# Loads two double pairs ahead, copies in the tick of their matmul, and a held-back second set in a long-convolution and FFN kernel

## The chip, the cores and the metric

The kernel runs on one core of a Trainium2 chip. The metric is the device time of one execution in microseconds (us); the profile shows one execution by its engines: TensorE (PE, its weight loads apart as PEld), VectorE (DVE), ScalarE (ACT), GpSimd (POOL), and the DMA issues of SyncE (SP) and GpSimd.

## The reference

For four sequences of 12480 positions and 128 channels, a long convolution by FFT is followed by a product and by a feed-forward network (FFN):

```python
h_filt = (np.maximum(pos_emb @ w1, 0.0) @ w2) * np.exp(-0.01 * np.arange(S))[:, None]
Uf = np.fft.rfft(x * v, n=2 * S, axis=1)
Hf = np.fft.rfft(h_filt, n=2 * S, axis=0)
y = np.fft.irfft(Uf * Hf[None], n=2 * S, axis=1)[:, :S]
t = (x * y).reshape(B * S, 128)
h = t @ w_in                      # 128 -> 2048
out = (h / (1 + np.exp(-1.702 * h))) @ w_out
```

## The kernel before

The transform is written as two stages of matmuls with constant matrices, and its inverse likewise. The work on the convolution comes in five sets (SETS: which block and which one or two of the sequences); set 0 also computes the filter's spectrum.

Stage 1 of a set takes 26 pairs of columns. For a pair it multiplies x and v (L226), computes two columns of the filter by a small network (mlp_in L192, Relu L194 into rt, mlp_out L200, product with the window L202), adds and subtracts (fold, L182 and L183), multiplies by a constant matrix (L242), copies the result from PSUM (a, L245) and stores it to the DRAM tensor g_d (g_out, L208). Two neighbouring pairs form a double pair and share their loads: x2 (L214), f2 (L217) and pt (L187).

Stage 2 of a set takes 31 steps v. A step loads two column groups from g_d (L315), multiplies by the small matrix wf (forward, L302), copies spectra to eu (L334), forms the products t1 and t2 on VectorE (L340) and y on GpSimd (L344, L345), multiplies by wv (inverse, L308), copies to z (L356) and stores to z_d (L357). Set 0's spectra are needed by the later sets. The eu tiles of the last KEEP steps have buffers of their own, and spec_store (L360, L361) writes them to DRAM after the loop; those of the first steps share two buffers and are stored in the loop.

The third part (p3_unit) loads z_d by GpSimd's queue (zt L456, vt L460, x3 L462), does the last inverse matmul (L482) and the product with x, and leaves the FFN's input as two parts xh and xl. The FFN runs over 104 halves (NH) of 8 steps. A step has six matmuls of 480 columns into h (L555), two Gelu passes (L556, L557), a subtraction (L563) and six matmuls into acc (L572).

What sets the order: the program order is written out by hand, each engine keeps it, and so does each DMA queue. A unit of work is a Python generator. One tick of a Pipe advances every live generator by one yield, the oldest first, and then the new one. So a statement that stands n yields deep in a generator is issued n ticks after its unit began. In the prologue there is one tick for each pair of stage 1 and each step of stage 2 of set 0, with five and nine empty ticks behind them, and every tick ends with two heat matmuls (L625, their result is unused). Buffers are rings: the n-th tile of a tag takes the place of the (n - bufs)-th and waits for its last reader. All wide PSUM results of set 0 take a ring of three (cv2), and the small network has a single bank.

After the prologue the other sets are fed between the FFN's steps by Feed: every unit has a weight, pace(k, span) sets the weight per step so that a mark (the end of a set) is reached in span steps, and run(steps) issues units up to that goal. `begin[0]` is the step at which the first half of set 1 needs its z_d, 96. Ahead of the first FFN step six ticks of the third part run.

The pools of the prologue (st, and keep for the eu tiles) are closed behind it, and the pools of the FFN (ffn) and of the fed sets (main) take that memory.

Of the kernel before, what the change touches and what calls it, by code (L numbers as in the profile page):

```python
# [9 lines left out]
F32 = mybir.dt.float32  # L10
F32R = mybir.dt.float32r
U32 = mybir.dt.uint32
ACTF = mybir.ActivationFunctionType
# [11 lines left out]
M = HALF // N2  # L25
K1 = N1 // 2 + 1
KP = 128
KZ = 122
NP = N2 // 2
# [4 lines left out]
WCH = 512  # L34
LAG = 4
STEPS = FC // 2
KEEP = 22

PAIRS = [(n, N2 - n) for n in range(1, NP)] + [(0, NP)]
SETS = [(0, 0, 1), (0, 1, 1), (0, 2, 2), (1, 0, 2), (1, 2, 2)]  # L40
# [72 lines left out]
def conv_ffn_kernel(  # L113
# [45 lines left out]
    def sb(name, shape, dt, bufs, tag=None, where="s"):  # L159
        return ps[where].tile(shape, dt, tag=tag or name, bufs=bufs, name=name)  # L160
# [15 lines left out]
    def flat(t):  # L176
        return t.rearrange("p a b c -> p (a b c)")
# [7 lines left out]
    def mlp_load(j, p):  # L185
        pt = sb("pt", [128, 2 * M], F32, 2)
        nc.sync.dma_start(out=pt, in_=posm[:, j, p // 2])  # L187
        return pt
# [16 lines left out]
    def g_out(j, p, a):  # L205
        for q in range(2):
            r = 64 * q + 2 * p
            nc.sync.dma_start(out=g_d[j][r:r + 2].rearrange("r k c -> k r c"), in_=a[:, :, q * 256:(q + 1) * 256])  # L208

    def p1_start(p):  # L210
        c, h = divmod(p, 2)
        if h == 0:
            x2 = sb("x2", [M, 2, 2, 2, 128], F32, 4, "g")
            nc.sync.dma_start(out=x2, in_=xv[:, 8 * c:8 * c + 8].rearrange("m (p x i) d -> m p x i d", p=2, x=2))  # L214
            f2 = sb("f2", [M, 3, 2, 128], F32, 2)
            n = 3 if p + 1 == LONE else 2
            nc.sync.dma_start(out=f2[:, 0:n], in_=c_f0[:, p:p + n])  # L217
            shared["in"] = x2, f2, mlp_load(0, p)
        x2, f2, pt = shared["in"]
        yield  # L220
        if h == 0:
            shared["rt"] = mlp_in(pt)
        rt = shared["rt"]
        yield
        u = sb("u", [M, 2, 2, 128], F32, 2)
        tt(out=u[:, :, 1], in0=x2[:, h, 0], in1=x2[:, h, 1], op=ALU.mult)  # L226
        mlp_out(u, rt, 0, p)
        yield
        if p == LONE:
            pq = u  # L230
        else:
            pq = sb("pq", [M, 2, 2, 128], F32, 2)
            fold(pq, u)
        yield
        t, bs = pair(True)
        for ri in range(2):
            if p == LONE:
                for q in range(2):
                    mm(out=bs[ri][:, q * 256:(q + 1) * 256], lhsT=f2[:, h + ri, q],
                       rhs=pq[:, ri].rearrange("p b c -> p (b c)"), start=True, stop=True)  # L240
            else:
                mm(out=bs[ri], lhsT=f2[:, h, ri], rhs=flat(pq), start=True, stop=True)  # L242
        yield
        a = sb("a", [KP, 2, 512], F32, 2)
        act(a, t, ACTF.Copy)  # L245
        yield
        g_out(0, p, a)

# [71 lines left out]
    def p2_start(v):  # L320
        nw = min(2, KZ // 2 - 2 * v)
        w0 = 2 * v
        wd = 128 * nw
        g = p2_load(0, v, nw)
        yield
        yield
        t, xy = pair(True)
        forward(g, nw, xy)
        yield
        keep = v >= NV - KEEP  # L330
        eu = sb("eu", [128, 2, 2, 2, 128], F32, KEEP if keep else 2, where="k" if keep else "s")
        tv = t[:, :, 0:256 * nw].rearrange("p l (w s c) -> p s w l c", w=nw, s=2)
        for s in range(2):
            act(eu[:, s, 0:nw], tv[:, s], ACTF.Copy)  # L334
        yield
        t1 = sb("t1", [128, 2, wd], F32, 2, "u")
        t2 = sb("t2", [128, 2, wd], F32, 2, "pq")
        pw = [128, 2, nw, 128]
        for i, to in enumerate((t1, t2)):
            tt(out=to.rearrange("p l (w c) -> p l w c", w=nw), in0=tv[:, 1].rearrange("p w l c -> p l w c"),  # L340
               in1=eu[:, 0, 0:nw, i].unsqueeze(1).broadcast_to(pw), op=ALU.mult)
        yield
        y = sb("y", [128, 2, wd], F32, 2)
        nc.gpsimd.tensor_tensor(out=y[:, 0], in0=t1[:, 0], in1=t2[:, 1], op=ALU.subtract)  # L344
        nc.gpsimd.tensor_tensor(out=y[:, 1], in0=t2[:, 0], in1=t1[:, 1], op=ALU.add)  # L345
        if keep:
            spectra.append((eu, w0, nw))
        else:
            spec_store(eu, w0, nw)
        yield  # L350
        yield
        t, ab = pair(True)
        inverse([y[:, i].rearrange("p (w c) -> p w c", w=nw) for i in range(2)], nw, wd, ab)
        yield
        z = sb("z", [128, 2, 2, 128], F32, 2)
        act(z[:, 0:nw].rearrange("p w a c -> p a w c"), t[:, :, 0:wd].rearrange("p a (w c) -> p a w c", w=nw), ACTF.Copy)  # L356
        nc.sync.dma_start(out=z_d[0][:, 4 * v:4 * v + 2 * nw, :], in_=z[:, 0:nw].rearrange("p w a c -> p (w a) c"))  # L357

    def spec_store(eu, w0, nw):
# [243 lines left out]
    with tc.manual_schedule():  # L603
        with tc.tile_pool(name="ps0", bufs=3, space=PSUM) as ps0, tc.tile_pool(name="ps0b", bufs=1, space=PSUM) as ps0b, \
                tc.tile_pool(name="st", bufs=1) as st, tc.tile_pool(name="keep", bufs=1) as kp:
            ps["s"], ps["k"] = st, kp
            ps["p"] = type("P", (), {"tile": staticmethod(
                lambda shape, dt, tag, name: (ps0 if tag == "cv2" else ps0b).tile(shape, dt, tag=tag, name=name))})
            warm = sb("warm", [128, 512], mybir.dt.bfloat16, 1)
            nc.vector.memset(warm, 0.0)  # L610
            zero = sb("zero", [128, KP - KZ, 256], F32, 1)
            nc.vector.memset(zero, 0.0)
            nc.vector.memset(w1_sb, 0.0)
            nc.vector.memset(w2_sb, 0.0)
            nc.vector.memset(sgn_sb[0:64], 1.0)
            nc.vector.memset(sgn_sb[64:128], -1.0)
            for h in range(2):
                nc.sync.dma_start(out=w1_sb[64 * h:64 * h + 64, 64 * h:64 * h + 64], in_=w1)
                nc.sync.dma_start(out=w2_sb[64 * h:64 * h + 64, h], in_=w2)
            nc.sync.dma_start(out=win_sb, in_=c_win)  # L620
            wb = ps0b.tile([128, 512], F32, tag="wb", name="wb")

            def heat(k):
                for _ in range(k):
                    mm(out=wb, lhsT=warm[:, 0:128], rhs=warm, start=True, stop=True)  # L625

            heat(24)
            pipe, wpipe = Pipe(), Pipe()
            wu = list(weight_units())
            units = [p1_start(p) for p in range(NP)] + [None] * 5  # L630
            units += [p2_start(v) for v in range(NV)] + [None] * 9
            for n, u in enumerate(units):
                pipe.tick(u)
                heat(2)
                if n == 4:
                    nc.sync.dma_start(out=wf, in_=c_wf)
                    nc.sync.dma_start(out=wv, in_=c_wi)
                    for o in range(5):
                        nc.sync.dma_start(out=z_d[o][:, KZ:KP], in_=zero[:, :, 0:128 * SETS[o][2]])
                if n >= 5:  # L640
                    wpipe.tick(wu.pop(0) if n % 6 == 5 and wu else None)
            assert not wu and not wpipe.live and not pipe.live
            for sp in spectra:
                spec_store(*sp)
# [9 lines left out]
        first = {next(i for i, hv in enumerate(HV) if hv[0] == o): o for o in range(1, 5)}  # L654
        begin = sorted(when(n) for n in first)
        feed = Feed(pipe, *conv_feed())
        feed.pace(0, begin[0])
        for n in range(6):
            p3.tick(p3_unit(0) if n == 0 else None)
            feed.run(1)  # L660
        ffn = Ffn()
        pend = []
        for n in range(NH):
            for k in range(STEPS):
                if pend:
                    ffn.lo(pend[-1])
                if len(pend) == LAG - 1 and pend[0][1] == STEPS - 1:
                    ffn.mm2(pend.pop(0))
                pend.append(ffn.mm1(n, k))
                feed.run(0.5)  # L670
                if n + 1 < NH:
                    new = None
                    if k == 0:
                        if n + 1 in first:
                            o = first[n + 1]
                            feed.reach()
                            if o < 4:
                                feed.pace(o, begin[o] - begin[o - 1] - 2)
                            else:
                                feed.rate = 0.0  # L680
                        new = p3_unit(n + 1)
                    p3.tick(new)
                if k == 4:
                    ffn.store()
                if len(pend) == LAG:
                    ffn.mm2(pend.pop(0))
                feed.run(0.5)
        ffn.lo(pend[-1])
        for it in pend:
            ffn.mm2(it)  # L690
# [124 lines left out]
```

## Time and profile before

| | |
|---|---|
| median of 3 runs | 3180.36 us (3177.92 to 3182.05) |
| profiled execution, time | 3184.23 us |
| profiled execution, span | 3182.5 us |
| mean granted TensorE clock | 0.972 |
| PE busy | 3025.1 us, 95% |
| DMA moved | 541.84 MB |
| SP queue's share of 16 DMA engines | 38.8% |
| GpSimd queue's share | 15.6% |

The span runs from the first to the last instruction. A busy share is a mean over stretches that differ much: the first 351 us hold set 0's two stages and the hand-over, the rest the FFN with the other sets fed between its steps. Matmuls are pipelined, so a busy PE may still be late by small amounts. A wait is put down to what ended last before the waiting instruction began.

### The profile page before, as it was taken

To read this page: it belongs to the slowest core of one execution; us is meant where nothing else is said; L and a number is where in the kernel's file an instruction comes from. 1 tells how busy PE (TensorE), PEld (TensorE's weight loads), DVE (VectorE), ACT (ScalarE), POOL (GpSimd) and SP (SyncE) were. 2 spreads that over 40 slices of the span, in tenths; PEclk is the share of its full clock that TensorE was granted. 3 is DMA by queue.
4 is the path that set the end of the run, shared out by engine and by line. 5 is a ranking of instruction groups with operands and counts; after the bars stand their busy time and mean duration, and the time that the engine had idled before them with its cause. 6 is when DMAs were issued, how large, how long until landed. Compare 5 with 4: busy or idle time off the path is not lost.

```text
span 3182.5 us, 42011 instructions
## 1 busy us (share of the span) xinstructions
PE 3025.1 (95%) x15191; PEld 2313.3 (73%) x15206; DVE 2156.1 (68%) x2874; ACT 2073.1 (65%) x2812; POOL 426.4 (13%) x694
## 2 busy tenths in 40 slices
PE   6764699999999999999999999999999999999999
PEld 3311587668866678877777887777777888888887
DVE  3452467777777776799998548888887444545444
ACT  1233576668877777766666766666666767666676
POOL 0033111012201011111111111111111111111110
PEclk7877899999999999999999999999999999999999
DMA  6676888889977797665656524544542111111110
GB/s 194 196 235 201 247 243 263 248 254 316 313 236 255 241 295 214 187 201 195 197 185 189 158 80 131 169 152 162 169 159 88 49 54 48 54 47 54 47 55 26
DMA packets 281799, 541.84 MB, mean 170 GB/s; under 512 B 30963, under 2 KB 149811, under 8 KB 281595
## 3 DMA queue, kind: packets, MB, share of 16 engines
q1 hardware_dynamic: 230603, 390.34, 38.8%
q0 software_dynamic: 50992, 148.82, 15.6%
q8 instruction: 123, 2.02, 0.3%
q14 instruction: 81, 0.66, 0.1%
HBM read 330.24 MB, written 208.80 MB: 169 GB/s over the span
## 4 chain that ended last, share of the span: by engine, by line
PE 43%; issue 39%; POOL 4%; DVE 2%; SPq 1%; DMA 1%; ACT 0%; POOLq 0%; DVEq 0%; ACTq 0%
PE acc L572 15%; PE h L555 15%; PE cv L302 3%; PE cv L482 3%; PE cv L308 2%; POOL zt L456 2%; PE cv L172 1%; PE cv L174 1%; PE cv L173 1%; POOL out_dram L583 1%; POOL x L462 1%; POOL vt L460 1%; SPq L360 1%; SPq L361 1%; DVE fgl L563 0%
## 5 line engine op out<-in xcount | busy, mean ns | idle before, releaser
L563 DVE TENSOR_TENSOR fgl<-fg,fgh 128x960 fp32r<-128x960 f32 x832 | 959.1, 1155 | 603.0 <-ACT fg L557 530.7
L556 ACT ACTIVATE fgh<-h 128x960 fp32r<-128x960 f32 x832 | 810.3, 974 | 587.7 <-PE h L555 586.4
L555 PE MATMUL h<-xh,wi 128*128 128x480 f32 x3328 | 1130.8, 383 | 0.0
L572 PE MATMUL acc<-fgh,wo 128*128 128x480 f32 x3328 | 884.8, 387 | 0.0
L557 ACT ACTIVATE fg<-h 128x960 f32<-128x960 f32 x832 | 807.1, 970 | 9.3 <-DVE fgl L563 9.2
L555 PEld LDWEIGHTS h<-xh,wi 128*128 128x128 f32 x3328 | 626.0, 188 | 184.4 <-issue 67.2
L572 PEld LDWEIGHTS acc<-fgh,wo 128*128 128x128 f32 x3328 | 609.6, 188 | 172.9 <-issue 86.0
L555 PE MATMUL h<-xl,wi 128*128 128x480 f32 x1664 | 632.2, 380 | 0.0
L572 PE MATMUL acc<-fgl,wo 128*128 128x480 f32 x1664 | 500.3, 382 | 1.7 <-DVE fgl L563 1.7
L572 PEld LDWEIGHTS acc<-fgl,wo 128*128 128x128 f32 x1664 | 312.8, 188 | 51.4 <-DVE fgl L563 2.1
L555 PEld LDWEIGHTS h<-xl,wi 128*128 128x128 f32 x1664 | 312.9, 188 | 47.4
L583 POOL DMA_DIRECT2D out_dram<-ot x104 | 57.1, 549 | 2009.8 <-ACT ot L576 2007.6
L482 PEld LDWEIGHTS cv<-vt,zt 122*128 122x128 f32 x1664 | 202.1, 193 | 20.8 <-ACT fg L557 6.5
L482 PE MATMUL cv<-vt,zt 122*128 122x120 f32 x1664 | 205.4, 277 | 2.5 <-DMA vt<-in_c_v_dram 1.6
L302 PE MATMUL cv<-g,wf 52*64 52x512 f32 (+1 forms) x1240 | 182.3, 640 | 9.1 <-DMA g<-g_d 4.9
L456 POOL DMA_DIRECT2D zt<-z_d x208 | 151.7, 735 | 15.5 <-DMA e_d<-eu 6.9
L440 ACT ACTIVATE z<-cv 128x512 f32<-128x512 f32 (+2 forms) x248 | 120.5, 545 | 41.7 <-PE cv L308 41.4
L492 DVE TENSOR_TENSOR a<-cv,yq 128x240 f32<-128x240 f32 (+1 forms) x101 | 40.7, 403 | 140.8 <-ACT yq L490 85.1
L295 ACT ACTIVATE a<-cv 128x512 f32<-128x512 f32 x208 | 120.9, 607 | 23.2 <-PE cv L174 21.3
L308 PE MATMUL cv<-t,wv 52*64 52x512 f32 (+2 forms) x992 | 126.2, 555 | 2.7 <-DVE e L420 1.7
L262 POOL DMA_DIRECT2D ft<-in_c_f_dram x108 | 57.5, 534 | 479.5 <-PE cv L174 444.7
L576 ACT ACTIVATE ot<-acc 128x480 f32<-128x480 f32 x104 | 59.5, 572 | 91.4 <-PE acc L572 91.4
(84 smaller groups left out, 2514.5 us busy)
## 6 DMA issues: line engine op xcount, KB each, us to landing
g_d<-a SPq DMA_DIRECT2D x260, 256.0 KB
g<-g_d SPq DMA_DIRECT2D x300, 208.0 KB
zt<-z_d POOLq DMA_DIRECT2D x208, 256.0 KB, 4.3
e<-e_d SPq DMA_DIRECT2D x180, 256.0 KB
z_d<-z SPq DMA_DIRECT2D x90, 512.0 KB
xt<-in_xv_dram SPq DMA_DIRECT2D x78, 480.0 KB
u<-us_d SPq DMA_DIRECT2D x60, 512.0 KB
ft<-in_c_f_dram POOLq DMA_DIRECT2D x108, 240.0 KB, 4.5
```

The lines of the kernel that those rows point to most:

```text
L295: act(a[:, ri], b, ACTF.Copy)
L302: mm(out=xy[q ^ c][64 * c:64 * c + 64, 0:256 * nw].rearrange("p (w c) -> p w c", w=nw), lhsT=wf[64 * q:64 * q + N2, c], rhs=g[64 * q:64 * ...
L308: mm(out=ab[h][64 * pl:64 * pl + 64, 0:w].rearrange("p (w c) -> p w c", w=nw), lhsT=wv[64 * h:64 * h + N2, pl], rhs=y[pl ^ h][64 * h:64 * ...
L440: act(zv[:, :, h], ab[h][:, 0:wd].rearrange("p (w c) -> p w c", w=nw), ACTF.Copy)
L456: q.dma_start(out=zv[:, gq], in_=z_d[o][64 * gq + 2 * p0:64 * gq + 2 * p0 + 2 * npr].rearrange("r k c -> k r c"))
L482: mm(out=b[:, c0:c0 + M], lhsT=lhs, rhs=rhs, start=(k == 0), stop=(k == 1))
L555: mm(out=h[:, i, 0:TW], lhsT=wt[:, s], rhs=xx, start=st, stop=sp)
L556: act(gh, h[:, :, 0:TW], ACTF.Gelu_apprx_sigmoid)
L557: act(gf, h[:, :, 0:TW], ACTF.Gelu_apprx_sigmoid)
L563: tt(out=gl, in0=gf, in1=gh.bitcast(F32), op=ALU.subtract)
L572: mm(out=acc, lhsT=wt[:, 2 * k + i, :], rhs=xx[:, i], start=(t == 0 and i == 0 and k == 0), stop=(t == 2 and i == 1 and k == STEPS - 1))
L583: nc.gpsimd.dma_start(out=out[:, n], in_=ot)
```

## The change

- Stage 1 of set 0: the loads of a double pair become p1_load and are issued AHEAD = 2 double pairs before their first use; two of them are issued ahead of the loop. pt is now loaded first. The rings: pt 3 in place of 2, f2 5 smaller ones in place of 2; the third matrix that the last pair needs gets a tile of its own, f3.
- The copy of a is issued in the tick of its matmul; its store stays in the tick where it was.
- Stage 2 of set 0: the copy to eu is issued in the tick of the forward matmul, and all that follows it one tick earlier; the copy to z is issued in the tick of the inverse matmul, and its store one tick after. z has three buffers in place of two.
- KEEP is 21 in place of 22, and the tile of zeros is one row that the stores to z_d broadcast six times.
- HOLD = 10: no unit of set 1 is issued in the six ticks ahead of the FFN and in its first ten steps, and set 1's pace is reckoned over 86 steps.

```diff
-KEEP = 22
+KEEP = 21
+AHEAD = 2
+HOLD = 10
...
+    def p1_load(c):
+        p = 2 * c
+        pt = sb("pt", [128, 2 * M], F32, 3)
+        nc.sync.dma_start(out=pt, in_=posm[:, 0, c])
+        x2 = sb("x2", [M, 2, 2, 2, 128], F32, 4, "g")
+        nc.sync.dma_start(out=x2, in_=xv[:, 8 * c:8 * c + 8].rearrange("m (p x i) d -> m p x i d", p=2, x=2))
+        f2 = sb("f2", [M, 2, 2, 128], F32, 5)
+        nc.sync.dma_start(out=f2, in_=c_f0[:, p:p + 2])
+        fl = [f2[:, 0], f2[:, 1]]
+        if p + 1 == LONE:
+            f3 = sb("f3", [M, 2, 128], F32, 1)
+            nc.sync.dma_start(out=f3, in_=c_f0[:, NP])
+            fl.append(f3)
+        shared["in", c] = x2, fl, pt
+
     def p1_start(p):
         c, h = divmod(p, 2)
-        if h == 0:
-            x2 = sb("x2", [M, 2, 2, 2, 128], F32, 4, "g")
...
-            f2 = sb("f2", [M, 3, 2, 128], F32, 2)
...
-            shared["in"] = x2, f2, mlp_load(0, p)
-        x2, f2, pt = shared["in"]
+        if h == 0 and c + AHEAD < NP // 2:
+            p1_load(c + AHEAD)
+        x2, fl, pt = shared["in", c]
         yield
...
-                mm(out=bs[ri], lhsT=f2[:, h, ri], rhs=flat(pq), start=True, stop=True)
-        yield
+                mm(out=bs[ri], lhsT=fl[h][:, ri], rhs=flat(pq), start=True, stop=True)
         a = sb("a", [KP, 2, 512], F32, 2)
         act(a, t, ACTF.Copy)
+        yield
         yield
         g_out(0, p, a)
...
         forward(g, nw, xy)
-        yield
         keep = v >= NV - KEEP
...
         inverse([y[:, i].rearrange("p (w c) -> p w c", w=nw) for i in range(2)], nw, wd, ab)
-        yield
-        z = sb("z", [128, 2, 2, 128], F32, 2)
+        z = sb("z", [128, 2, 2, 128], F32, 3)
         act(z[:, 0:nw].rearrange("p w a c -> p a w c"), t[:, :, 0:wd].rearrange("p a (w c) -> p a w c", w=nw), ACTF.Copy)
+        yield
         nc.sync.dma_start(out=z_d[0][:, 4 * v:4 * v + 2 * nw, :], in_=z[:, 0:nw].rearrange("p w a c -> p (w a) c"))
...
-            zero = sb("zero", [128, KP - KZ, 256], F32, 1)
+            zero = sb("zero", [128, 1, 256], F32, 1)
...
+            for c in range(AHEAD):
+                p1_load(c)
...
-        feed.pace(0, begin[0])
+        feed.pace(0, begin[0] - HOLD)
         for n in range(6):
             p3.tick(p3_unit(0) if n == 0 else None)
-            feed.run(1)
...
-                feed.run(0.5)
+                if n * STEPS + k >= HOLD:
+                    feed.run(0.5)
```

Both calls of feed.run(0.5) in an FFN step get the condition shown last.

More of the change, by code (lines that the diff above doesn't have):

```diff
@@ L208, in g_out @@
             nc.sync.dma_start(out=g_d[j][r:r + 2].rearrange("r k c -> k r c"), in_=a[:, :, q * 256:(q + 1) * 256])
+    def p1_load(c):
[12 more added lines that the diff above has]
+        shared["in", c] = x2, fl, pt
     def p1_start(p):
         c, h = divmod(p, 2)
-        if h == 0:
-            x2 = sb("x2", [M, 2, 2, 2, 128], F32, 4, "g")
-            nc.sync.dma_start(out=x2, in_=xv[:, 8 * c:8 * c + 8].rearrange("m (p x i) d -> m p x i d", p=2, x=2))
-            f2 = sb("f2", [M, 3, 2, 128], F32, 2)
-            n = 3 if p + 1 == LONE else 2
-            nc.sync.dma_start(out=f2[:, 0:n], in_=c_f0[:, p:p + n])
-            shared["in"] = x2, f2, mlp_load(0, p)
-        x2, f2, pt = shared["in"]
+        if h == 0 and c + AHEAD < NP // 2:
+            p1_load(c + AHEAD)
+        x2, fl, pt = shared["in", c]
         yield
@@ L238, in p1_start @@
                 for q in range(2):
-                    mm(out=bs[ri][:, q * 256:(q + 1) * 256], lhsT=f2[:, h + ri, q],
+                    mm(out=bs[ri][:, q * 256:(q + 1) * 256], lhsT=fl[h + ri][:, q],
                        rhs=pq[:, ri].rearrange("p b c -> p (b c)"), start=True, stop=True)
             else:
-                mm(out=bs[ri], lhsT=f2[:, h, ri], rhs=flat(pq), start=True, stop=True)
-        yield
+                mm(out=bs[ri], lhsT=fl[h][:, ri], rhs=flat(pq), start=True, stop=True)
         a = sb("a", [KP, 2, 512], F32, 2)
         act(a, t, ACTF.Copy)
+        yield
         yield
@@ L353, in p2_start @@
         inverse([y[:, i].rearrange("p (w c) -> p w c", w=nw) for i in range(2)], nw, wd, ab)
+        z = sb("z", [128, 2, 2, 128], F32, 3)
+        act(z[:, 0:nw].rearrange("p w a c -> p a w c"), t[:, :, 0:wd].rearrange("p a (w c) -> p a w c", w=nw), ACTF.Copy)
         yield
-        z = sb("z", [128, 2, 2, 128], F32, 2)
-        act(z[:, 0:nw].rearrange("p w a c -> p a w c"), t[:, :, 0:wd].rearrange("p a (w c) -> p a w c", w=nw), ACTF.Copy)
         nc.sync.dma_start(out=z_d[0][:, 4 * v:4 * v + 2 * nw, :], in_=z[:, 0:nw].rearrange("p w a c -> p (w a) c"))
@@ L638, in conv_ffn_kernel @@
                     for o in range(5):
-                        nc.sync.dma_start(out=z_d[o][:, KZ:KP], in_=zero[:, :, 0:128 * SETS[o][2]])
+                        nc.sync.dma_start(out=z_d[o][:, KZ:KP], in_=zero[:, :, 0:128 * SETS[o][2]].broadcast_to([128, KP - KZ, 128 * SETS[o][2]]))
                 if n >= 5:
@@ L686, in conv_ffn_kernel @@
                     ffn.mm2(pend.pop(0))
-                feed.run(0.5)
+                if n * STEPS + k >= HOLD:
+                    feed.run(0.5)
         ffn.lo(pend[-1])
```

## The prediction

> **What bounds the kernel now.** I read the page's head first, then busy time by stretches, then the waits of the early stretches, then the timeline where those waits sit. A wait row is engine, line, what it waited for, then total us, times, longest.
>
> ```profile
> span 3182.5 us, 42011 instructions
> PE 3025.1 (95%) x15191; PEld 2313.3 (73%) x15206; DVE 2156.1 (68%) x2874; ACT 2073.1 (65%) x2812; POOL 426.4 (13%) x694
> ```
>
> ```profile
> 12.00:142.00 130.00, 88.59 (x204) 43.10 (x208) 54.68 (x134) 27.05 (x36) 0.00 (x0) 0.79 0.66 200
> 162.00:291.00 129.00, 86.50 (x548) 23.40 (x556) 64.21 (x102) 51.18 (x94) 48.02 (x62) 0.76 0.66 203
> 291.00:351.00 60.00, 11.18 (x47) 8.01 (x46) 5.67 (x14) 4.32 (x10) 7.50 (x12) 0.59 0.92 280
> 351.00:760.00 409.00, 405.08 (x2138) 304.05 (x2137) 295.91 (x513) 294.81 (x484) 57.72 (x98) 1.00 0.86 257
> 700.00:800.00 100.00, 98.35 (x492) 81.07 (x491) 77.59 (x132) 78.43 (x124) 20.31 (x36) 1.00 1.00 307
> 2600.00:2800.00 200.00, 200.00 (x988) 174.49 (x987) 96.83 (x106) 139.07 (x167) 27.46 (x45) 1.00 0.16 52
> ```
>
> The columns are stretch, its length, busy PE, PEld, DVE, ACT, POOL, granted clock, DMA share, GB/s. From 351 us on PE is full at clock 1.00, so nothing there can be gained without less matmul work, and the change removes none. Ahead of it lie 351 us in three stretches where neither PE nor the DMA is full: stage 1 of set 0 (12 to 142), its stage 2 (162 to 291), and 60 us with 11 us of PE. Whatever brings the FFN's first matmul forward brings the end forward by as much. The rows of waits of the three stretches, in that order:
>
> ```profile
> PE cv L192 <- DMA pt<-in_posm_dram: 37.0, 10, 8.6
> ACT a L245 <- DMA g_d<-a: 21.1, 8, 10.4
> ...
> ACT eu L334 <- DMA us_d<-eu: 29.0, 7, 5.8
> DVE t L340 <- POOL y L345: 37.3, 20, 2.9
> PE cv L308 <- DVE t L340: 25.4, 16, 3.5
> ...
> PE cv L192 <- DMA xt<-in_xv_dram: 46.8, 1, 46.8
> ```
>
> **Stage 1: loads two double pairs ahead.** One double pair in the timeline, and the row of L192 for the whole run:
>
> ```profile
> 72.97 0.36 SPq L217 DMA_DIRECT2D f<-in_c_f_dram  x1
> 73.38 0.39 SPq L187 DMA_DIRECT2D pt<-in_posm_dram  x1
> ...
> 76.37 1.14 PE L192 MATMUL cv<-pt,w_sb 128*128 128x240 f32 x2 [3.00 <-DMA pt<-in_posm_dram]
> 78.16 2.59 PE L242 MATMUL cv<-pq,f 120*128 120x512 f32 x4
> 81.45 1.88 PE L242 MATMUL cv<-pq,f 120*128 120x512 f32 x4
> 83.17 0.60 PE L200 MATMUL cv<-w_sb,rt 128*120 128x256 f32 x2
> 87.00 1.14 PE L192 MATMUL cv<-pt,w_sb 128*128 128x240 f32 x2 [3.24 <-DMA pt<-in_posm_dram]
> ...
> L192 PE MATMUL cv<-pt,w_sb x26: 366/607/767, 12.2 to 142.6; 128*128 128x240 f32 x26
> ```
>
> The f2 load (L217) has a ring of two, so it waits for the L242 of two double pairs earlier; pt is issued behind it at 73.38 and lands 3.0 us later, and L192 of the same tick waits for it. That is the 37.0 us. After the change pt stands first and is issued two double pairs (some 14 us) early, and every ring slot taken (pt 3, x2 4, f2 5) was released a tick before: the wait goes. What is late next? PE itself from 76.37 to 83.77 takes 7.4 us, and L192 must wait about 0.6 us (an estimate: L202 and two hand-overs) for the one bank that L200's reader releases: 8.0 us for 10.6 now. L242 is slow (2.59) right behind the 3 us hole and fast (1.88) later; with both ticks fast PE needs about 6.3. The DMA was busy 0.66 of 130 us = 86 us for 12 double pairs, 7.2 each, and this becomes the bound. I take 94 us (91% DMA) for the 130: **-36 us**; ends 86 (-44) and 115 (-15, rival B). The Trainium skill (TensorE: Matmul & The Clock Gate, Part 1: The HAM clock gate) says that the clock falls to half after an idle window of about 3.4 us. The trace agrees, with 2.59 against 1.88 us behind a hole of 3.0. By that rule a hole of 0.6 us keeps the clock full; without it the stage would take 12 times 8.0 = 96 us.
>
> SP is moved past too: three loads per double pair now stand ahead of two g_out pairs, but as many issues as before (some 0.4 us each). The copy of a moves ahead of rt in its tick, where it runs under the L200 and L192 that follow L242: nothing. The store of a stays in its tick, so the ring of two a's loses its spare tick: rival B. The zero fill sends the same bytes in smaller pieces on a DMA that is 0.66 busy; I put it at nothing, at most 2 us, and it costs that where the DMA is full.
>
> **Stage 2: copies and products a tick earlier.** The first four rows are from its first third, where the spectra are spilled; the next four from the end:
>
> ```profile
> L302 PE MATMUL cv<-g,wf x248: 589/631/1112, 161.7 to 284.3; 52*64 52x512 f32 x120, 52*64 52x256 f32 x4
> ...
> 188.23 1.09 ACT L334 ACTIVATE eu<-cv 128x512 f32<-128x512 f32 x2 [5.83 <-DMA us_d<-eu]
> 189.20 0.60 ACT L356 ACTIVATE z<-cv 128x512 f32<-128x512 f32 x1
> 190.69 0.45 SPq L361 DMA_DIRECT2D us_d<-eu  x1
> 194.19 1.09 ACT L334 ACTIVATE eu<-cv 128x512 f32<-128x512 f32 x2 [4.39 <-DMA us_d<-eu]
> ...
> 279.24 0.66 PE L308 MATMUL cv<-y,wv 52*64 52x256 f32 x8 [1.64 <-DVE t L340]
> 280.06 0.73 POOL L344 TENSOR_TENSOR y<-t,t 128x256 f32<-128x256 f32 x1 [2.29 <-issue]
> 281.50 1.29 DVE L340 TENSOR_TENSOR t<-cv,eu 128x512 f32<-128x512 f32 x2 [2.41 <-POOL y L345]
> 282.94 1.13 PE L308 MATMUL cv<-y,wv 52*64 52x256 f32 x8 [1.43 <-DVE t L340]
> ```
>
> Spilling ticks run a ring of one tick: eu, z, SP's store of z, the store of eu behind it, its landing, the next eu: 188.23 to 194.19, 6.0 us. With z copied a tick before its store, SP no longer stands on a copy that follows eu, and the ring spans two ticks: 3.0 each. Their data (g 0.42, z 0.26, spectra 0.52 MB by the tile shapes) at the 280 to 307 GB/s of the full stretches needs about 4.2, which is what I take, ten times (KEEP 21 spills one more), 42 us. Later ticks run L308, y (its ring of two waits for L308), t (waits for y), and L308 again, which takes the PSUM slot that t releases in that tick: 3.7 us. With t a tick earlier the slot is free a tick earlier and this ring too spans two ticks, 1.9 each; the data (0.68 MB) needs 2.3, so 2.6 for 21 ticks, 55 us. With 7 us of start and drain that is 104 us for the 129.6 from 161.7 to 291.27 (below): **-25 us**. Ends: the DMA's 0.66 of 129 = 85 us plus the tenth spill, -40; the old rings with only the spill mended, -8. DVE (64 of 129 us) and PE (86.5, at clock 0.76) fit under 104.
>
> **Hand-over and HOLD.** In order of time, then the landing row of vt and the ACT busy time of L557 by itself (one per FFN step) in the late stretch:
>
> ```profile
> 291.27 0.45 PE L308 MATMUL cv<-y,wv 52*64 52x128 f32 x8
> 297.85 1.67 POOL L456 DMA_DIRECT2D zt<-z_d x2 [6.93 <-DMA e_d<-eu]
> 331.69 0.73 SPq L361 DMA_DIRECT2D us_d<-eu  x1
> 334.54 0.37 SPq L254 DMA_DIRECT2D xt<-in_xv_dram  x1
> 339.91 1.14 PE L192 MATMUL cv<-pt,w_sb 128*128 128x240 f32 x2 [46.79 <-DMA xt<-in_xv_dram]
> 340.85 3.60 PE L482 MATMUL cv<-vt,zt 122*128 122x120 f32 x16
> 350.84 0.60 PE L555 MATMUL h<-xh,wi 128*128 128x480 f32 x1
> ...
> DMA to landing us min/median/max: 5.9/7.3/8.8
> ...
> 2600.00:2800.00 200.00, 67.85 (x70) 1.00 0.16 52
> ```
>
> PE stood 46.8 us on a matmul of the second set, whose loads were queued on SP behind 44 spectra stores, while the FFN's own inputs (zt, vt on POOL) were issued at 297.85 and landed by about 308. With HOLD no matmul of the second set stands ahead: L482 can start 1.67 + 8.8 = 10.5 us behind the zt issue, and L555 some 6.5 us later (3.60 of its own and about five passes of 0.6; between 3.6 and the 10.0 shown). So 17 us from zt to L555 for 53.0: **-36 us**. The third z buffer takes out a wait for a z store near 292: **-2.5** (0 to -4). Given back: the second set's matmuls that ran between 339.91 and 350.84, about 7 us at half clock, now fall into the full stretch: **+3.5**.
>
> The held steps cost nothing: 200 / 70 = 2.86 us a step, all PE, and the feed's PE work is the same later. Ten are 29 us, by which time SP (stores until about 38 us behind the last L308, feed from 21 + 29 = 50) is free. The second set then has 86 steps in place of 96 plus six early ones, and six steps less of slack at the thirteenth half: 352 us of DMA (0.86 of 409) go into about 373. The cover is that PE stays full at a DMA share of 1.00, where 700 to 800 shows 1.65 us idle: **+2** (0 to +8).
>
> **Sum**: -36 - 25 - 36 - 2.5 + 3.5 + 2 = -94. The profiled execution took 3184.2 us, 3.9 above the median of the runs (3180.4): 3090 against it, 3086 against the median; I forecast 3088. All ends together give 3057 and 3136.
>
> **Rivals.**
> B, stage 1 stays behind its stores. Copies of a already wait 21.1 us for g_d stores, with a spare tick that now goes, and 0.9 MB of loads go ahead of each odd store; ACT is in order, so rt and then L200 wait. If that keeps a double pair at about 9.2, the stage takes 115: 3109. Against it: by the rows above rt is needed only behind another L242 and a heat pass, some 3 us later. [...]
> C, stage 2 stays on landings (z and eu stores, g loads on a full DMA): 3.4 us a late tick, 120 us: 3104.
> D, a buffer of the FFN lies on spectra memory and waits for their stores: L555 near 331 on the old clock (334.54 less the shorter tail and two stores) instead of 312: 3107. Only 44 stores ending before any FFN work are in the trace, so it can't show this.
> E, slower: the denser second set fills the DMA and PE stands on its loads up to step 96. To undo more than 94 us, 352 us of DMA would have to become 467 in 373. PE at 98.35 of 100 with share 1.00 speaks against it; 3190.
>
> **Chances.** Forecast 0.62 (3068 to 3106 by itself), B 0.15, D 0.09, C 0.08, two of these together 0.03 (3130), E 0.02, about nothing 0.01. The range 3064 to 3120 leaves out little more than E, the pairs and the tails of the terms. The runs shown spread over 0.13%, so under 0.2% (6 us) counts as no change: faster 0.96, same 0.01, slower 0.03.
>
> **What the next profile would show.** No wait of L192 for pt and L192 running from about 12 to 106; the first L302 near 126 and the last L308 near 230; L482 about 15 us behind the last L308, no xt wait of tens of us; L555 near 251; PE full from there. L192 spaced over 9 us with a waiting for g_d is B; L308 still waiting for t is C; L555 behind the last L361 is D; PE holes before the thirteenth half are E. I am wrong at large if the stretches run into a full DMA at less than 280 GB/s.

## The result, and the profile after

The median fell from 3179.54 us (3177.92 to 3182.05) to 3084.34 us (3080.99 to 3086.50): a ratio of 0.9699, 95% interval 0.9682 to 0.9716. The forecast was 3088 (3064 to 3120). The profiled execution took 3084.36 us, as long as the median, where that of before (3184.23) stood 4.7 us above its own; so differences between the two profiles come out about 5 us larger than those between medians.

The page's head, and the stretches that answer to those of before (the lines of the source have moved: L194 was L192, L254 was L242, L256 was L245, L314 was L302, L320 was L308, L345 was L334, L351 was L340, L493 was L482, L566 was L555):

```profile
span 3082.6 us, 42056 instructions
PE 3000.9 (97%) x15206; PEld 2303.4 (75%) x15206; DVE 2159.1 (70%) x2874; ACT 2071.1 (67%) x2812; POOL 430.5 (14%) x694
```

```profile
8.00:102.00 94.00, 70.77 (x213) 34.35 (x211) 53.27 (x131) 27.24 (x37) 0.00 (x0) 0.93 0.94 284
119.00:211.00 92.00, 77.57 (x560) 19.95 (x562) 68.79 (x104) 51.77 (x96) 52.21 (x62) 0.90 0.88 291
211.00:230.00 19.00, 5.95 (x32) 4.32 (x32) 1.38 (x3) 1.41 (x4) 7.53 (x12) 0.64 0.97 337
231.00:643.00 412.00, 404.94 (x2122) 302.87 (x2123) 288.66 (x501) 287.04 (x471) 55.41 (x94) 0.99 0.88 261
```

The three early stretches took 130, 129 and 60 us and take 94, 92 and 19. In all of them the DMA share is now 0.88 to 0.97. PE is busy for 0.75 and 0.84 of the first two stretches, so these shares alone do not say whether the transfers or PE bound them. The granted clock of stage 1 is 0.93 for 0.79. The fourth stretch holds the FFN's first 96 steps; PE is busy in 404.94 of its 412 us.

The waits, stage 1 first, then stage 2, then the hand-over:

```profile
ACT a L256 <- DMA g_d<-a: 48.3, 12, 16.0
PE cv L202 <- ACT rt L196: 16.4, 3, 14.3
...
ACT eu L345 <- DMA us_d<-eu: 15.9, 6, 3.6
PE cv L320 <- ACT z L366: 8.4, 5, 2.8
...
PE cv L493 <- DMA vt<-in_c_v_dram: 10.5, 1, 10.5
```

No wait for pt, none of L320 for t, and none for xt at the hand-over is left among the long ones. The waits for spectra stores halved (29.0 to 15.9), and one has grown: the copies of a wait 48.3 us for their stores (21.1 before), once for 16.0.

Landmarks, from the rows of L194, L314 and the timeline:

```profile
L194 PE MATMUL cv<-pt,w_sb x26: 366/366/470, 8.5 to 102.1; 128*128 128x240 f32 x26
...
L314 PE MATMUL cv<-g,wf x248: 376/589/1114, 118.6 to 206.7; 52*64 52x512 f32 x120, 52*64 52x256 f32 x4
...
210.92 0.45 PE L320 MATMUL cv<-y,wv 52*64 52x128 f32 x8
215.74 1.67 POOL L467 DMA_DIRECT2D zt<-z_d  x2 [5.17 <-DMA z_d<-z]
223.75 3.74 PE L493 MATMUL cv<-vt,zt 122*128 122x120 f32 x16 [10.55 <-DMA vt<-in_c_v_dram]
230.16 0.77 PE L566 MATMUL h<-xh,wi 128*128 128x480 f32 x1 [2.67 <-ACT xh L510]
```

| | before | after | shift so far |
|---|---|---|---|
| last L192/L194 of stage 1 | 142.6 | 102.1 | -40.5 |
| first forward matmul | 161.7 | 118.6 | -43.1 |
| last inverse matmul | 291.3 | 210.9 | -80.4 |
| zt issue | 297.9 | 215.7 | -82.2 |
| first FFN matmul | 350.8 | 230.2 | -120.6 |
| end of the span | 3182.5 | 3082.6 | -99.9 |

So 120.6 us were won ahead of the FFN, and 20.7 of them were given back behind its first matmul. The FFN's steps show where, taken from the first Gelu pass (L556 before, L567 after) of one step to that of another: steps 0 to 96 took 407.1 us and take 408.5, steps 96 to 304 took 787.0 and take 805.5, the rest took 1622.5 and takes 1622.6. Nearly all of it is given back behind step 96.

### The profile page after: what moved, and what is told of

Read it like the earlier page. It is cut to its first block, busy times and chain, and to the rows that moved or that the text cites. A ratio compares the mean times of both kernels' runs of the same rounds, so it can differ in the third digit from the quotient of the medians.

```text
span 3082.6 us, 42056 instructions
## 1 busy us (share of the span) xinstructions
PE 3000.9 (97%) x15206; PEld 2303.4 (75%) x15206; DVE 2159.1 (70%) x2874; ACT 2071.1 (67%) x2812; POOL 430.5 (14%) x694
## 4 chain that ended last, share of the span: by engine, by line
PE 42%; issue 41%; POOL 5%; DVE 4%; DMA 2%; ACT 1%; POOLq 0%; SPq 0%; DVEq 0%; ACTq 0%
PE acc L583 14%; PE h L566 14%; PE cv L314 3%; PE cv L320 3%; PE cv L493 3%; POOL zt L467 2%; PE cv L174 1%; PE cv L175 1%; PE cv L176 1%; DVE fgl L574 1%; DMA vt<-in_c_v_dram 1%; POOL out_dram L594 1%; POOL x L473 1%; POOL vt L471 1%; DVE t L417 0%
## 5 line engine op out<-in xcount | busy, mean ns | idle before, releaser
L567 ACT ACTIVATE fgh<-h 128x960 fp32r<-128x960 f32 x832 | 810.3, 974 | 586.7 <-PE h L566 585.9
L566 PE MATMUL h<-xh,wi 128*128 128x480 f32 x3328 | 1133.2, 384 | 3.4 <-ACT xh L510 2.7
L568 ACT ACTIVATE fg<-h 128x960 f32<-128x960 f32 x832 | 807.1, 970 | 14.3 <-DVE fgl L574 13.9
L566 PEld LDWEIGHTS h<-xh,wi 128*128 128x128 f32 x3328 | 626.4, 188 | 191.0 <-issue 70.6
L566 PE MATMUL h<-xl,wi 128*128 128x480 f32 x1664 | 632.6, 380 | 0.0
L566 PEld LDWEIGHTS h<-xl,wi 128*128 128x128 f32 x1664 | 313.1, 188 | 47.2 <-DVE xl L512 0.4
L493 PEld LDWEIGHTS cv<-vt,zt 122*128 122x128 f32 x1664 | 204.8, 195 | 34.3 <-issue 16.2
L493 PE MATMUL cv<-vt,zt 122*128 122x120 f32 x1664 | 208.0, 279 | 16.8 <-DMA vt<-in_c_v_dram 16.8
L314 PE MATMUL cv<-g,wf 52*64 52x512 f32 (+1 forms) x1240 | 177.9, 623 | 11.2 <-DMA g<-g_d 4.9
L320 PE MATMUL cv<-t,wv 52*64 52x512 f32 (+2 forms) x992 | 128.7, 555 | 5.3 <-DVE e L431 4.0
L307 ACT ACTIVATE a<-cv 128x512 f32<-128x512 f32 x208 | 119.4, 608 | 19.6 <-PE cv L176 18.7
```

The source lines that it names most:

```text
L307: act(a[:, ri], b, ACTF.Copy)
L314: mm(out=xy[q ^ c][64 * c:64 * c + 64, 0:256 * nw].rearrange("p (w c) -> p w c", w=nw), lhsT=wf[64 * q:64 * q + N2, c], rhs=g[64 * q:64 * ...
L320: mm(out=ab[h][64 * pl:64 * pl + 64, 0:w].rearrange("p (w c) -> p w c", w=nw), lhsT=wv[64 * h:64 * h + N2, pl], rhs=y[pl ^ h][64 * h:64 * ...
L493: mm(out=b[:, c0:c0 + M], lhsT=lhs, rhs=rhs, start=(k == 0), stop=(k == 1))
L566: mm(out=h[:, i, 0:TW], lhsT=wt[:, s], rhs=xx, start=st, stop=sp)
L567: act(gh, h[:, :, 0:TW], ACTF.Gelu_apprx_sigmoid)
```

## The experiments

Each ratio is to the kernel before, timed on the same chip. The median of the kernel before lay between 3179.5 and 3181.0 us in all rounds, so a difference to the changed kernel (its runs: 3081.0 to 3086.5) carries an uncertainty of a few us. Five profiled executions have the changed stage 1 as it is (the changed kernel, e1, e4, e6, e9); in them the last L194 begins at 101.9 to 104.1 us, and that is the spread against which stage 1 is judged below. The first four kernels take the change apart.

**e1, stage 1's part alone.** The changed kernel with stage 2 and the feed put back:

```diff
         forward(g, nw, xy)
+        yield
...
-        feed.pace(0, begin[0] - HOLD)
+        feed.pace(0, begin[0])
...
+            feed.run(1)
```

> Stage 1's part alone: the loads two double pairs ahead and the copy of a in the tick of its matmul (with KEEP 21, the smaller zero tile); stage 2 and the feed as before. Theory S (the stretches before the FFN stand in series, each part moves its own): L192's last run about 40 us earlier, the first FFN matmul near 310 on its span, the end 38 to 42 us earlier (about 3140), PE idle behind the FFN's start as before (about 6 us). Rival O (a fuller DMA in stage 1 only pushes stores into stage 2, which then takes longer): under 25 us (over 3155), stage 2 longer than its 130 us.

Measured: 3136.05 us (ratio 0.9862, 0.9847 to 0.9876), 45 us less than before. L194 ends at 102.4 and the last inverse matmul stands at 245.86, so that stage 2 was not made longer by a fuller DMA ahead of it (119.0 to 245.9, 127 us for 130). The first FFN matmul moved 48.5 us (302.3), the end 48.8: nothing given back. O falls; S holds in kind, with 45 us for its 38 to 42.

**e2, stage 2's part alone.** The kernel before with the three edits of stage 2, and with the one-row tile of zeros (not shown):

```diff
         forward(g, nw, xy)
-        yield
...
-        yield
-        z = sb("z", [128, 2, 2, 128], F32, 2)
+        z = sb("z", [128, 2, 2, 128], F32, 3)
         act(z[:, 0:nw]...
+        yield
```

> Stage 2's part alone: the copy to eu in the tick of the forward matmul, the products a tick earlier, the copy to z in the tick of the inverse matmul, three z buffers (with the smaller zero tile); stage 1 and the feed as before. Theory S: the stretch from the first forward matmul to the last inverse one takes about 93 us instead of 130, the end comes 36 to 40 us earlier (about 3142). Rival O (the rings of a tick go, but the landings of stores and loads take their place unless stage 1 has been shortened too): 105 us or more, under 25 us of gain (over 3155).

Measured: 3141.49 us (0.9878, 0.9862 to 0.9895), 39.5 less. From the row of its forward matmuls and its last inverse one in the timeline:

```profile
L302 PE MATMUL cv<-g,wf x248: 376/589/1112, 156.9 to 245.0; 52*64 52x512 f32 x120, 52*64 52x256 f32 x4
...
249.21 0.45 PE L308 MATMUL cv<-y,wv 52*64 52x128 f32 x8
```

Stage 2 takes 156.9 to 249.2 = 92.3 us without any help from stage 1, just as long as in the whole change (118.6 to 210.9 = 92.3). So theory S holds, and these edits are the whole of stage 2's gain. That they work through the two rings fits the spacing of the forward matmuls, read from the timelines of the kernel before and after: it was 3.7 us in most of the late steps and is 2.6 on average and 2.0 in the last ones, near the 1.9 of a ring that spans two ticks.

**e3, HOLD alone,** on the kernel before:

```diff
+HOLD = 10
-        feed.pace(0, begin[0])
+        feed.pace(0, begin[0] - HOLD)
...
-            feed.run(1)
...
-                feed.run(0.5)
+                if n * STEPS + k >= HOLD:
+                    feed.run(0.5)
```

> HOLD alone, on the kernel before. The 46.8 us wait for xt goes. Theory G1 (what HOLD gives at the hand-over is given back in part, because the second set has 86 steps and no slack: PE waits on transfers and DVE, and its clock falls behind the longest waits): the first FFN matmul about 38 us earlier, the end only 15 to 25 us earlier (3155 to 3165), PE idle behind the FFN's start 12 us or more. Rival G2 (only the feed matmuls that ran before the FFN, some 6 us, move behind its start): the end 30 to 34 us earlier (about 3148), PE idle as before (6 us).

Measured: 3157.82 us (0.9932, 0.9917 to 0.9946), 23.2 less. The first FFN matmul comes at 303.9 for 350.8, 46.9 earlier, the end of the span (3154.9) only 27.6: 19.3 given back. About 5 of the 46.9 us lie ahead of the hand-over, where HOLD changes nothing (last inverse matmul at 286.1 for 291.3); the hand-over itself is 41.8 shorter. The steps of the FFN show the same as in the whole change: 408.5 us for steps 0 to 96, 804.2 for 96 to 304. So the give-back belongs to HOLD, as theory G1 had it.

**e4, the change without HOLD:**

```diff
-        feed.pace(0, begin[0] - HOLD)
+        feed.pace(0, begin[0])
...
+            feed.run(1)
...
-                if n * STEPS + k >= HOLD:
-                    feed.run(0.5)
+                feed.run(0.5)
```

> The changed kernel without HOLD: stage 1 and stage 2 as changed, the feed as before. Theory S with G1: the wait for xt is back (some 45 us of PE), the first FFN matmul near 271, no give-back, the end about 3100: HOLD nets 15 to 20 us though it moves the FFN by 38. With G2 HOLD nets about 32 and this run takes about 3116. Rival O: the sum of the three parts alone misses the whole by over 15 us.

Measured: 3099.83 us (0.9748, 0.9733 to 0.9762), 81.2 less. S with G1 had about 3100. The old wait stands again at the hand-over, and nothing is given back (first FFN matmul 264.1, 86.7 earlier; end 87.4 earlier):

```profile
PE cv L194 <- DMA xt<-in_xv_dram: 39.8, 1, 39.8
```

On medians, stage 1 and stage 2 give 45.0 + 39.5 = 84.5 alone and 81.2 together: they stand in series. HOLD gives 23.2 alone and 3099.83 - 3084.34 = 15.5 on top. The difference lies in the hand-over: from the last inverse matmul to the first FFN matmul it takes 59.6 us before and 17.8 in e3, but 53.5 in e4 and 19.2 in the whole change. There was less left to take away, as in e4 the last spectra store is issued 31.4 us behind the last inverse matmul and not 40.4 as before. Stage 2's edit is not the main cause of that: with it alone (e2) the distance is 38.1, with e1's edits (KEEP 21 among them, two stores fewer) 33.1. Which of e1's edits does it was not separated.

**e5, the zero fill later.** The changed kernel's stage 1 has one long hole: L194 runs every 6.4 to 7.9 us, but once after 22.7. The timeline of the changed kernel there:

```profile
22.69 3.52 SPq L652 DMA_DIRECT2D z_d<-zero  x2
35.76 1.02 ACT L256 ACTIVATE a<-cv 128x1024 f32<-128x1024 f32 x1 [16.02 <-DMA g_d<-a]
42.05 1.21 PE L202 MATMUL cv<-w_sb,rt 128*120 128x256 f32 x2 [14.28 <-ACT rt L196]
```

The reading to be tested: the fill's 3.1 MB go out at once, the stores of a behind it land late, the copy of a waits for its ring of two, rt waits behind the copy on ACT, and PE for rt. The edit:

```diff
-                    for o in range(5):
+                    for o in range(1):
                         nc.sync.dma_start(out=z_d[o][:, KZ:KP], in_=zero...
...
             for sp in spectra:
                 spec_store(*sp)
+            for o in range(1, 5):
+                nc.sync.dma_start(out=z_d[o][:, KZ:KP], in_=zero...
```

> The changed kernel with the zero fill of sets 1 to 4 (2.7 MB of 3.1) moved from stage 1 to behind the spectra stores; set 0's stays. Theory Z (in the changed kernel stage 1 lost one long wait: the fill puts 10 us of DMA work at once ahead of the stores of a, the copy of a waits 16 us on its ring of two, rt behind it on ACT, then PE): the 22.7 us spacing of L194 falls to 6 to 8, stage 1 ends about 15 us earlier, the end 8 to 15 us earlier (3070 to 3076). Rival D (stage 1 is bound by the DMA's 0.97 busy share; the wait is only where the fill shows): the 9 us of DMA time come off and no more in stage 1, but are paid back in stage 2 or at the hand-over: within 4 us of 3084.

Measured: 3114.49 us (0.9798, 0.9785 to 0.9812): 30 us slower than the changed kernel, which neither theory had. Stage 1 and 2 did become shorter (last inverse matmul near 203.8 for 210.9), but the hole only went from 22.7 to 15.9: most of the fill is gone from there and a good part of the hole is not. And then:

```profile
POOL zt L467 <- DMA xt<-in_xv_dram: 40.9, 1, 40.9
PE cv L493 <- DMA pt<-in_posm_dram: 48.4, 1, 48.4
```

Neither name can be the cause; zt reads no xt. What the zt load must wait for is the memory that it is written to. That asks for e10.

**e10, the zeros in a tile that lives on.** e5 with one line more:

```diff
-            zero = sb("zero", [128, 1, 256], F32, 1)
+            zero = const.tile([128, 1, 256], F32, name="zero")
```

> The changed kernel with the zero fill of sets 1 to 4 behind the spectra stores, as in e5, and the tile of zeros in the pool that lives through the whole kernel. Theory M (in e5 zt of the FFN took the memory of the zeros' tile and so waited for the stores behind the spectra, 48 us of PE): that wait goes, the first FFN matmul comes near 222, and with the shorter stage 1 and 2 of e5 (inverse done at 204 instead of 211) the end is 4 to 9 us earlier than 3084 (3075 to 3080). Rival (late fills hold the queues up by themselves): the wait of L493 stays over 20 us and the end over 3095.

Measured: 3078.49 us (0.9677, 0.9664 to 0.9690). The wait of zt is gone and PE's is that of the landing again:

```profile
219.57 3.74 PE L493 MATMUL cv<-vt,zt 122*128 122x120 f32 x16 [11.48 <-DMA vt<-in_c_v_dram]
```

Theory M holds: the late stores are still there, only the tile's place has changed, and the wait is gone. So in e5 the FFN's zt took the memory of the prologue's tile of zeros and stood behind stores that were queued behind all spectra. The mechanism of the prediction's rival D exists, then; in the change itself no such pair of tiles is late. Against the changed kernel the gain of some 6 us is close to the width of the intervals.

**e6, HOLD 6:**

```diff
-HOLD = 10
+HOLD = 6
```

> The changed kernel with HOLD 6: the feed starts four steps (11 us) earlier, near the end of the spectra stores, and set 1 has 90 steps. Theory G1 (give-back by missing slack in sets 1 and 2): PE idle behind the FFN's start falls from 17.7 us by a third or more, the end 2 to 6 us earlier. Rival: the first loads of the second set now stand behind the last spectra stores on SP and PE waits for them: a wait of L194 of 3 to 8 us, the end the same or later by up to 5 us.

Measured: 3078.14 us (0.9683, 0.9670 to 0.9696). The intervals of the two ratios overlap, so the 6 us are not clear of noise; the two profiles differ by only 3.9 us. From the first FFN matmul to the end it takes 2849.8 us for 2852.4, and PE is idle there for 24.3 us for 25.1 (15.5 in the kernel before). Steps 0 to 96 take 406.3 us and steps 96 to 304 take 805.2: the loss behind step 96 is as large as with HOLD 10. The time is in the range of G1, but G1 in the form of "a few steps more" is not borne out; the expected wait behind the spectra stores is there, but small (1.6 us once).

**e7, AHEAD 1:**

```diff
-AHEAD = 2
+AHEAD = 1
```

> The changed kernel with AHEAD 1. If one double pair ahead (6.4 us at the new pace) covers the landing of pt and x2: the same within 3 us, the spacing of L194 stays at 6.4. If loads need longer on a DMA that is 0.97 busy, PE waits for pt or DVE for x again, 1 to 3 us a double pair: 10 to 30 us slower (3095 to 3115).

Measured: 3078.08 us (0.9682, 0.9669 to 0.9696). One double pair ahead covers the loads: spacing 6.4. It is not slower but rather faster by some 6 us: the last L194 begins at 96.4, clear of the 101.9 to 104.1 above, with the hole at the zero fill 19.3 us for 22.7. That fewer loads stand ahead of the stores of a would explain it; it was not tested apart.

**e8, three buffers of a:**

```diff
-KEEP = 21
+KEEP = 20
...
-        a = sb("a", [KP, 2, 512], F32, 2)
+        a = sb("a", [KP, 2, 512], F32, 3)
```

> The changed kernel with three buffers of a in stage 1 (and KEEP 20, one more spectrum stored inside stage 2). Rival B of the prediction (copies of a wait for their stores): with a third buffer the waits of the copy of a for g_d (44.4 us between 10 and 100) fall to under 15, and stage 1 shortens by 5 to 12 us, most of it at the zero fill. If the DMA's share alone sets the pace: stage 1 within 3 us of 93.6, the end the same.

Measured: 3075.46 us (0.9676, 0.9663 to 0.9689), 9 us faster than the changed kernel. The last L194 begins at 95.1 for 102.1; the hole is 18.7, and behind it the spacing is 6.4 throughout. The copies' wait is nearly halved between 10 and 100 us (24.8 for 44.4, where under 15 was expected):

```profile
ACT a L256 <- DMA g_d<-a: 24.8, 5, 13.7
```

**e12, the copy of a back in the tick behind its matmul,** the loads as changed:

```diff
+        yield
         a = sb("a", [KP, 2, 512], F32, 2)
         act(a, t, ACTF.Copy)
-        yield
         yield
         g_out(0, p, a)
```

> The changed kernel with stage 1's copy of a put back to the tick behind its matmul; loads two double pairs ahead as changed. If the copy's place is worth nothing by itself (it runs as soon as its matmul has ended, and ACT has little to do): within 3 us of 3084, spacing of L194 6.4. If the earlier place matters because the store of a can go out before the next loads: stage 1 longer by 10 us or more (over 3092). If it hurts, since rt now stands behind copies that wait for their stores: faster by 4 us or more.

Measured: 3076.83 us (0.9672, 0.9659 to 0.9686), 7.5 us less than the changed kernel (the runs of the two, 3072.5 to 3081.2 and 3081.0 to 3086.5, all but part; the intervals of the ratios overlap a little). The last L194 begins at 96.7, clear of 101.9 to 104.1; its hole at the fill is 19.4, and its spacing behind that 6.4 without the 7.9 and 7.4 us that the changed kernel shows. So this part of the change hurts, by some 5 us of stage 1. That fits rt standing on ACT behind copies that wait for their stores: PE's wait at L202 for rt is 10.1 us for 16.4.

**e9, slack in the feed's pace:**

```diff
-        feed.pace(0, begin[0] - HOLD)
+        feed.pace(0, begin[0] - HOLD - 6)
...
-                                feed.pace(o, begin[o] - begin[o - 1] - 2)
+                                feed.pace(o, begin[o] - begin[o - 1] - 6)
```

> The changed kernel with slack put back into the feed's pace: set 1 reckoned over 80 steps instead of 86, the later sets to end six steps early instead of two. The kernels with HOLD give back 20 to 21 us behind the FFN's first matmul, 6 of it moved matmuls. Theory G1 (the other 14 are waits of PE at the ends of sets 1 and 2, where the z_d of a set comes just in time, and the clock behind them): the waits of L493 for vt near 722 and 1088 go, PE idle falls from 17 to 10 us or less, the end 4 to 9 us earlier (3075 to 3080). Rival (they are the DMA's: its work is denser whatever the pace): idle stays at 14 us or more, the end within 3 us of 3084 or later.

Measured: 3066.61 us (0.9642, 0.9629 to 0.9655), 17.7 less than the changed kernel. The waits of PE between FFN start and about step 304, first in the changed kernel and then in e9:

```profile
PE cv L493 <- DMA vt<-in_c_v_dram: 6.2, 3, 4.0
PE cv L320 <- DVE e L431: 4.0, 3, 1.5
```

```profile
PE cv L320 <- DVE e L431: 2.4, 2, 1.3
PE cv L320 <- ACT us L427: 1.7, 3, 0.6
```

No wait of L493 for vt is left. PE is idle for 5.9 us of these steps, as in the kernel before (5.9), and for 15.0 in the changed kernel (the stretch and PE's busy time in it, first the changed kernel, then e9):

```profile
232.00:1448.00 1216.00, 1200.97 (x6171) 901.69 (x6170) 930.50 (x1337) 871.48 (x1297) 167.12 (x282) 1.00 0.81 249
233.00:1436.00 1203.00, 1197.11 (x6191) 898.53 (x6189) 940.73 (x1351) 871.07 (x1299) 166.94 (x282) 1.00 0.82 254
```

By steps (from first Gelu pass to first Gelu pass, us):

| steps | before | changed | e3 | e6 | e9 |
|---|---|---|---|---|---|
| 0 to 96 | 407.1 | 408.5 | 408.5 | 406.3 | 414.3 |
| 96 to 304 | 787.0 | 805.5 | 804.2 | 805.2 | 786.5 |

The whole loss behind step 96 comes back. The gain of 17.7 is well over the 4 to 9 us that were expected, and the rival (the transfers' density, whatever the pace) falls. The code shows what e9 has in common with the kernel before. There the six early ticks made the feed reach set 1's mark at step 90, and it went on into set 2 from there; e9 reaches the mark at step 90 too, the changed kernel and e6 only at step 96. So it is not the number of steps that counts but that the feed is ahead of the mark. e9 also gives the later sets four steps more of slack, and the two were not run apart. Part of the feed's matmuls now lie earlier, so the split by steps shifts as well: steps 0 to 96 take 6 us longer than in the changed kernel, those behind 304 some 5 us less. From the first FFN matmul to the end e9 takes 2833.6 us, 1.9 more than the kernel before; the 14 matmuls of the second set that ran ahead of the FFN before run inside it now (the prediction put them at 3.5 us), so no loss beyond them is left.

**e11, all together:** three a with KEEP 20, AHEAD 1, the fill of e10, the slack of e9.

```diff
-KEEP = 21
-AHEAD = 2
+KEEP = 20
+AHEAD = 1
...
-        a = sb("a", [KP, 2, 512], F32, 2)
+        a = sb("a", [KP, 2, 512], F32, 3)
...
-            zero = sb("zero", [128, 1, 256], F32, 1)
+            zero = const.tile([128, 1, 256], F32, name="zero")
...
-        feed.pace(0, begin[0] - HOLD)
+        feed.pace(0, begin[0] - HOLD - 6)
...
```

> Three buffers of a with KEEP 20, AHEAD 1, the late zero fill from a tile of its own, and the slack of e9, HOLD 10. If the gains add (9 for the third a with part of the zero fill's in it, 4 for the fill, 3 for AHEAD 1, 5 for the slack): 3062 to 3068. If they are one and the same gain (stage 1's one long wait, taken away in several ways): 3070 to 3075.

Measured: 3048.12 us (0.9590, 0.9568 to 0.9612), 36 us less than the changed kernel and the best of all. It lies below both expected ranges, above all since e9's slack gave 17.7 us and not the 5 that was put in. Its profiled execution, at 3063.24 us, is 14 to 20 us longer than its other runs (3043.1 to 3049.0), with a granted clock of 0.95 where PE is full. Even so the last L194 begins at 85.6, its spacing 6.6 without a hole:

```profile
L194 PE MATMUL cv<-pt,w_sb x26: 374/375/470, 9.0 to 85.6; 128*128 128x240 f32 x26
```

The gain is e9's 17.7 and some 18 us ahead of the FFN, where the last inverse matmul comes 17.7 us earlier (193.2 for 210.9). AHEAD 1, the third buffer and the late fill had each taken 3 to 7 us out of the hole at the zero fill (19.3, 18.7 and 16.0 for 22.7), and two of them the 7 to 8 us spacings behind it; together they took all of the hole. So these gains about add, up to the size of the hole.

## Why the prediction was right, point by point

- **Stage 1: the wait went as forecast; the length was met in part by luck.** From the first L194 to the last it took 130.4 us and takes 93.6, where 94 was forecast. (It also begins 3.7 us earlier, so its end moved by 40.5; the sum had no term for that, nor for the 2.6 us won between the last L194 and the first forward matmul.) The wait for pt (37.0 us) is gone. But the bound that I took, 7.2 us of DMA for a double pair, 94 us with a margin, did not hold: the steady spacing is 6.4 (6.3 of PE by my working), with PE busy in 42.08 of the 48 us from 50 to 98 and a DMA share of 0.96. Twelve of these make 77 us; one hole of 22.7 us at the zero fill made up the rest. I had put that fill at no more than 2 us on account of its smaller pieces and never asked what its 3.1 MB would do to the queue. e5 and e10 put the fill's own part of the hole at some 7 us.
- **The clock.** The granted clock of stage 1 rose from 0.79 to 0.93, and 1.00 in the steady part; the median L194 takes 366 ns (607 before). The Trainium skill's rule on the idle window (TensorE: Matmul & The Clock Gate, Part 1: The HAM clock gate) gave 6.3 against 8.0 us for a double pair, and the trace agrees with the first (6.4). The prediction's own row agreed less well than it says: the hole in front of the slow L242 was 3.0 us, shorter than the window that the rule names, and the last section has a half clock right behind a wait of 1.28 us. So here a wait shorter than that window was no guarantee of a full clock.
- **Rival B happened, at one place.** Copies of a waited 48.3 us for stores, rt behind them and PE behind rt, as the rival put it; but PE's part was 16.4 us, 14.3 of it at the zero fill. e8, e7 and e12 bear out the chain: a third buffer, fewer loads ahead of the store, or rt ahead of the copy each shorten it. "Runs under the L200 and L192 that follow L242: nothing" was wrong for the copy of a: its earlier place costs some 5 us (e12).
- **Stage 2: the term was mis-sized.** -25 forecast, -37.3 measured (129.6 to 92.3). The edits that break the two rings were the cause, as e2 shows by itself. The late ticks came as forecast, 2.6 us on average. What was mis-sized was the spilling ticks, 3.5 on average for 4.2 (35 us for 42), and start and drain (4.5 us behind the last forward matmuls for 7). 92.3 lies inside the ends that I gave.
- **The hand-over: right.** zt to the first FFN matmul 53.0 to 14.4 us, -38.6 for -36; the tail to zt -1.8 for -2.5. HOLD does that by itself (e3: from the last inverse matmul to the first FFN matmul 59.6 to 17.8).
- **What HOLD gives back: the step that failed.** I reckoned +3.5 for moved matmuls and +2 for waits; it is +20.7. The sum looked for lost slack only up to the thirteenth half, step 96, and up to there it was nearly right: 1.4 us are lost. The 18.5 us lie in steps 96 to 304, where I put nothing. "PE stays full at a DMA share of 1.00" does not hold there: the z_d of a set comes just in time, and PE waits at L493 for vt (rows above), with the granted clock at one half behind some of these waits. e9 takes the loss behind step 96 away by pace alone, and e6, with four steps more but no slack at the mark, does not; so the missing slack and not the amount of transfers was the cause. How much of the 18.5 us is waiting and how much the clock and matmuls that moved behind step 96 was not separated. Rival E is not this: it put the holes before the thirteenth half.
- **The sum was right because two errors met.** Ahead of the FFN 120.6 us were won for 99.5 forecast, behind it 20.7 were lost for 5.5. On the profiles that is -99.9 for -94, on medians -95.2. That is luck: of the 21 us won beyond the forecast ahead of the FFN, 12 are stage 2's, 6 the earlier start and the stretch between the stages that had no term, and 3 the hand-over's; the 15 us more that were lost behind it come from another step of the sum and happened to cancel most of them.

## What to carry to other kernels

When a ring of buffers and the order of issue make each tick wait for the one before, moving one statement by a tick can shorten the tick much (here a late step of stage 2 from 3.7 us to 2.6 on average and 2.0 at best); find such a ring in the timeline by following one instruction until the same instruction comes again, and count the ticks that it spans. A bulk transfer can hold up small stores that a short ring of buffers waits for, so ask of each (here a zero fill of 3.1 MB, of which 2.7 were needed some 600 us later) what stands behind it in its queue, and before moving it, whose memory its tile will hand on. And work that is held back must get its slack again: what HOLD won at the hand-over was half given back at the deadlines (19.3 of 41.8 us in e3), until the pace was set to end early.

## What the runs showed of the hardware that I had not expected

- PE's granted clock stood at one half right behind short waits too. In the changed kernel L320 waited 1.28 us (to 546.25), and from about 547.4 to 550.8 the granted clock was one half while PE was full (rows of the stretches, then a later wait):

```profile
540.00:547.00 7.00, 5.71 (x34) 3.56 (x33) 4.18 (x8) 4.28 (x9) 3.12 (x5) 1.00 0.83 249
547.00:551.00 4.00, 4.00 (x17) 3.66 (x18) 1.26 (x2) 2.44 (x4) 0.00 (x0) 0.57 0.93 272
1088.56 3.74 PE L493 MATMUL cv<-vt,zt 122*128 122x120 f32 x16 [3.98 <-DMA vt<-in_c_v_dram]
```

  Around the wait of 3.98 us that ends at 1088.6 it was one half as well, from about 1087 to 1093.5, and L493 took 3.74 us, where a full clock gave 1.94 (at 706.5 in the kernel before). The same wait of 1.28 us in the kernel before (to 704.5), in e3 (to 620.0) and in e9 (to 551.6) had no such effect: the granted clock stayed at 1.00. What tells them apart stays open.
- One execution of e11 had a granted clock of 0.95 in every stretch in which PE was full (mean 0.942, its other runs 0.991 to 0.993), with one core at work. It was 14 to 20 us longer than the others. That is 0.5 to 0.7%, much less than a clock lower by 5% would make of a full PE; why stays open.
- With loads of GpSimd's queue beside the SP queue's stores the DMA moved 337 GB/s over 19 us (the hand-over row), more than the 280 to 307 that I had taken as its full rate. Two queues are not needed for that: in e11's stage 1, with no load on GpSimd's queue, it moved 332 GB/s over 67 us (15 to 82).
